# Which partitions the 64-feature rests are loaded into, in a linear-attention block with a gated feed-forward

## The chip, the cores and the metric

The kernel runs on one core of one Trainium2 chip. The metric is the device time of one execution in microseconds: 1095.71 us is the median of three runs before the change (1095.61 to 1099.36). The profile is of one further execution, taken by the hardware profiler.

## What is computed

x has 2048 tokens of 576 features. The reference, cut to what matters:

```python
xn = layernorm(x)
# A: linear attention, 32 heads of 18
q, k, v = split(xn @ wqkv)
pq, pk = phi(q), phi(k)             # phi(t) = t + 1 or exp(t), plus 1e-6
kv = einsum("bhsd,bhse->bhde", pk, v);  z = sum over s of pk
s = (pq @ kv) / (pq @ z + 1e-6) @ wo
# B: feed-forward, 576 -> 4608 -> 576
h = gelu(xn @ w1 + b1)
g = silu(h @ w2 + b2)
out = x + s * g
```

## The kernel before

Phase 1 (0 to about 190 us) normalizes x, multiplies it by wqkv and gathers the attention state. A hand-over (about 190 to 256 us) finishes the attention output of ten of the sixteen 128-token tiles and brings the main loop's first operands into SBUF. The main loop is the feed-forward, in two halves of 1024 tokens and, in each half, nine chunks of 512 hidden features. A short tail multiplies the last chunk and writes the output.

**Products.** Every large matrix product is made as seven block products with sums of blocks (the scheme of Strassen and Winograd); they are numbered 1 to 7 in the code. Each operand is held as a high part that the matmul unit takes exactly and a low part with what is left, so a product over 128 input features is three matmuls (high by high, high by low, low by high). The 576 input features of xn @ w1 are 4 x 128 and a rest of 64, which the block scheme cuts into two rests of 32. For a rest one matmul does all four combinations of high and low: 32 features x 2 parts of x x 2 parts of the weight fill the 128 partitions exactly. In class Up, product i of a pair of hidden blocks is six matmuls over X and a seventh whose moving operand is RX[:, RX_AT[i]] (the rest of x, 512 tokens wide) and whose stationary operand is a 128-column slice of we (the rest of w1); all seven are at line 1571 of the profile.

**The rests in DRAM.** The rests are split once, during phase 1 and the hand-over, and written to DRAM: rq_dram[half, i] holds for each product 32 features x (high, low) x 512 values, that is 64 rows of 2 KB; we_dram holds for each pair of hidden blocks 32 features x (high, low) x 896 values, rows of 3584 bytes. Each row goes to two partitions, so that each part of x meets each part of the weight. Before the change the upper 64 partitions of RX repeat the lower 64 (partition 64w + 2r + v holds feature r, part v of x), and the weights have part w in the 64 partitions from 64w on, each row on two neighbours. The tensor names in the profile are RX, we, rq_dram and we_dram.

**Who loads what, in which order.** All transfers are issued by SyncE (SP in the profile), one after the other in the order of the program; a transfer whose condition isn't met holds up all that are behind it. The engines' instructions are kept in the order written. The places that matter here:

- load_we (line 1346) issues two transfers of 224 KB for each pair of hidden blocks, 36 times. The first is called ahead of the hand-over's loop, right behind the load of w2raw (line 1301), the second in beside(7). In the main loop a table of steps (28 steps for each chunk) says when each call is made.
- load_rest (line 1455) is called from load_x_rest. In beside(5), within the hand-over, it is called for two tiles of RX and then for five; behind it stand the second load of w1raw (line 1362) and stores. At the change of half load_x_next loads for each of the seven products the X block of the second half (line 1888, 1 MB) and then its RX tile, one tile per call.
- load_q (line 1181) brings back a tile of q for the attention output: by_sums (line 1101, POOL) and p_mult (line 1116, POOL) work on it, then TensorE transposes (line 1252) and multiplies it (line 1287, ps_s).
- W1Loaded (line 1418) loads split blocks of w1 as wa, wc and wd in the second half; W2.load (line 1663) loads split blocks of w2, with one buffer each, so that its transfer waits until TensorE has done with the block of the chunk before (line 1733, pm).

Of the kernel before, what the change touches and what calls it, by code (L numbers as in the profile page):

```python
# [8 lines left out]
F32 = mybir.dt.float32  # L9
# [38 lines left out]
def linear_attention_gated_ffn(ctx, tc, x, xT, wqkv, wo, w1, w1e, b1, w2, b2, out):  # L48
    nc = tc.nc
# [65 lines left out]
    rq_dram = dram.tile([2, 8, 32, 2, 512], F32, name="rq_dram")  # L115
# [1222 lines left out]
    def load_we(n):  # L1338

        we_sb[n] = w1p.tile([P, WB, P], F32R, tag="we", name=f"we_{n}", bufs=2)  # L1340
        dst = we_sb[n].bitcast(F32).rearrange("p b c -> p (b c)")
        g, q = divmod(n % NP, WG)
        src = we_dram[q, 32 * g : 32 * g + 32]
        row = WB * P
        for w in range(2):
            nc.sync.dma_start(
                dst[64 * w : 64 * w + 64],
                bass.AP(
                    tensor=src.tensor, offset=src.offset + w * row,
                    ap=[[2 * row, 32], [0, 2], [1, row]],  # L1350
                ),
            )
# [97 lines left out]

    def load_rest(half, at, n, dst):

        src = rq_dram[half, at : at + n].rearrange("k r v c -> (r v) k c")
        for w in range(2):
            nc.sync.dma_start(dst[64 * w : 64 * w + 64].bitcast(F32), src)

    RX_AT = {i: at - (at > 2) for i, at in REST_AT.items()}

# [15 lines left out]
    def load_x_rest(half, i, n=1):  # L1474
        load_rest(half, REST_AT[i], n, RX[:, RX_AT[i] : RX_AT[i] + n])

    def beside(j):
        for half, what, *k in RESTS.get(j, ()):
            if half not in rests:
                rests[half] = Rest(half)  # L1480
            getattr(rests[half], what)(*k)
        if j == 2:
            nc.sync.dma_start(zb_dram, zb[0])
        if j == 4:
            w1t[0].hi("a"), w1t[0].lo("a")
        if j == 5:
            load_x_rest(0, 2, 2), load_x_rest(0, 4, 5)
            w1t[1] = W1(1)
            for i in (5, 6, 7, 4):
                w1t[0].T(i)  # L1490
        if j == 6:
            w1t[0].hi(6), w1t[0].lo(6)
            w1t[0].hi("c"), w1t[0].lo("c")
        if j == 7:
            load_we(1)
            w1t[0].hi("d"), w1t[0].lo("d")
# [9 lines left out]
    load_q(7)  # L1506
    w2_raw0.append(load_w2_raw(0))
    load_we(0)
    for j in range(NA):
        attend(j)  # L1510
# [541 lines left out]
    for step in range(n_chunks):  # L2052
        half, c = divmod(step, NC)
# [15 lines left out]
        if half == 0:  # L2069
# [7 lines left out]
            if (c, 5) not in w2_dram:  # L2077
                w = w2t[step]
# [5 lines left out]
        if not plain:  # L2084
            for k, at in enumerate((11, 16) if change else (8, 20) if step == NC else (7, 14)):
                add(base + at, load_we, 2 * step + 2 + k)
# [9 lines left out]
        elif not plain:  # L2096
            at = (11, 11, 16) if change else (7, 10, 24) if step == NC else (7, 14, 14)
# [7 lines left out]
            else:  # L2105
                make(W2, w2t, step + 1)

                w = w2t[step + 1]
# [42 lines left out]
        for j in range(CF // 2):  # L2151
            n = 2 * step + j
# [74 lines left out]
```

## Time and profile before

| | us |
|---|---|
| median of 3 runs | 1095.71 (1095.61 to 1099.36) |
| the profiled execution, its own time | 1107.71 |
| span in its profile, first to last instruction | 1105.9 |
| TensorE busy (PE) | 1084.5 |
| TensorE weight load busy (PEld) | 995.1 |
| VectorE busy (DVE) | 818.8 |
| ScalarE busy (ACT) | 524.8 |
| GpSimd busy (POOL) | 511.9 |

Mean granted TensorE clock 0.995; 258.63 MB moved, 234 GB/s in the mean. The profile has a page (busy time, the span in 40 slices, DMA queues, the chain of work that ended last, the costliest groups of instructions, DMA issues) and views that answer questions about the trace: waits, stretches of time, the chain in order of time, instructions in order of time. A line such as `PE a L1571 <- DMA wa<-op_a: 2.2, 1, 2.2` reads: TensorE, at line 1571, writing a, stood idle until a transfer from op_a to wa had landed; 2.2 us in all, once, 2.2 us the longest. `SPq` lines are the issues of transfers by SyncE; their time is that of the issue, not of the transfer. In the chain a `DMA` piece lasts from the issue to the landing.

### The profile page before, as it was taken

Reading aid. Unit: us, or ns where it says so; the run is one execution under the profiler, and the core shown is the slowest. Engines: PE = TensorE matmul, PEld = TensorE weight load, DVE = VectorE, ACT = ScalarE, POOL = GpSimd, SP = SyncE. Lnnn points to the kernel's source line nnn. Section 1 sums busy time; section 2 is a strip of 40 time slices with the busy share of each in tenths; the row PEclk is TensorE's granted clock in tenths of the full one; section 3 lists DMA queues with packets and bytes.
Section 4 is the critical chain, followed back from the end, with each engine's and each line's share of the span. In section 5 each row is a group of like instructions: output and inputs, shape, how many; then the busy total and the mean of one; then the engine's idle time right before and its main releaser. Section 6 shows DMA issues by size and latency. Waiting matters only on the chain.

```text
span 1105.9 us, 17916 instructions
## 1 busy us (share of the span) xinstructions
PE 1084.5 (98%) x6492; PEld 995.1 (90%) x6492; DVE 818.8 (74%) x1207; ACT 524.8 (47%) x872; POOL 511.9 (46%) x536
## 2 busy tenths in 40 slices
PE   8999999989999999999999998999999999999998
PEld 7999999788988989889899897989989899999988
DVE  6987763766898988989889884666747475664856
ACT  6756665635454554544545544244534434242442
POOL 3133241565585675765856743253334435252340
PEclk9999999999999999999999999999999999999999
DMA  6679733799577685685765799887767667676753
GB/s 235 192 277 230 232 117 134 248 339 350 193 245 283 205 299 204 224 291 199 283 243 202 262 290 338 290 273 230 219 208 225 200 212 224 186 236 207 233 157 137
DMA packets 91184, 258.63 MB, mean 234 GB/s; under 512 B 12246, under 2 KB 25558, under 8 KB 88792
## 3 DMA queue, kind: packets, MB, share of 16 engines
q1 hardware_dynamic: 91096, 257.49, 70.9%
q8 instruction: 51, 0.84, 0.3%
q14 instruction: 37, 0.30, 0.1%
HBM read 155.16 MB, written 101.40 MB: 232 GB/s over the span
## 4 chain that ended last, share of the span: by engine, by line
PE 89%; DMA 7%; ACT 2%; DVE 1%; POOL 1%; issue 1%; SPq 0%; POOLq 0%; DVEq 0%; ACTq 0%
PE pm L1733 32%; PE a L1571 10%; PE e L1571 10%; PE zy L1571 10%; PE b L1571 5%; PE x L390 4%; PE xaall L390 4%; PE pd L1854 2%; PE x1all L390 2%; PE psa L1287 2%; DMA X<-x_dram 1%; PE ps_kva L473 1%; DMA w2raw<-w 1%; PE x0all L390 1%; PE ps_s L1287 1%; PE xakv L390 1%
## 5 line engine op out<-in xcount | busy, mean ns | idle before, releaser
L1670 POOL TENSOR_TENSOR g<-g 128x256 f32<-128x256 f32 x204 | 185.4, 939 | 60.7 <-DVE h_l L1329 53.8
L1739 DVE TENSOR_TENSOR macc<-pm,macc 128x576 f32<-128x576 f32 x218 | 163.8, 751 | 47.7 <-PE pm L1733 47.2
L1326 ACT CAST h_h<-g 128x512 fp32r<-128x512 f32 x204 | 122.8, 621 | 123.3 <-PE pm L1733 122.2
L1329 DVE TENSOR_TENSOR h_l<-g,h_h 128x512 fp32r<-128x512 f32 x204 | 165.1, 816 | 2.4 <-ACT h_h L1326 2.3
L1571 PE MATMUL a<-X,wa 128*128 128x512 f32 x432 | 111.4, 394 | 2.2 <-DMA wa<-op_a 2.2
L1571 PEld LDWEIGHTS a<-X,wa 128*128 128x128 f32 x432 | 80.4, 190 | 18.1 <-ACT g L1579 2.6
L1588 ACT COPY mid<-a 128x512 f32<-128x512 f32 x36 | 21.1, 585 | 115.2 <-PE a L1571 115.2
L1670 POOL TENSOR_TENSOR mid<-g 128x256 f32<-128x256 f32 x68 | 52.2, 788 | 46.1 <-ACT g L1579 45.0
L1591 DVE TENSOR_TENSOR mid<-b,mid 128x512 f32<-128x512 f32 x36 | 24.8, 690 | 65.6 <-PE b L1571 59.0
L1377 POOL TENSOR_TENSOR w1raw<-w1raw 128x256 f32<-128x256 f32 x18 | 13.3, 741 | 117.1 <-ACT h_h L1326 71.6
L1579 ACT ACTIVATE g<-b,b1c 128x512 f32<-128x512 f32 x36 | 24.8, 689 | 66.9 <-DVE b L1597 66.9
L1571 PE MATMUL zy<-X,wd 128*128 128x512 f32 x216 | 55.0, 390 | 1.3 <-DMA X<-x_dram 1.3
L1571 PE MATMUL e<-X,wc 128*128 128x512 f32 x216 | 55.6, 392 | 0.0
L1571 PE MATMUL zy<-X,wc 128*128 128x512 f32 x216 | 54.8, 389 | 0.0
L1571 PE MATMUL e<-X,wd 128*128 128x512 f32 x216 | 54.8, 389 | 0.0
L1571 PEld LDWEIGHTS zy<-X,wd 128*128 128x128 f32 x216 | 40.5, 188 | 10.2 <-DMA X<-x_dram 1.7
L274 POOL TENSOR_TENSOR R<-R,bc 128x640 f32<-128x640 f32 x9 | 15.9, 1779 | 71.9 <-DMA R<-xT 48.5
L1571 PEld LDWEIGHTS zy<-X,wc 128*128 128x128 f32 x216 | 40.5, 188 | 8.4
L1571 PEld LDWEIGHTS e<-X,wd 128*128 128x128 f32 x216 | 40.5, 188 | 8.4
L1571 PEld LDWEIGHTS e<-X,wc 128*128 128x128 f32 x216 | 40.0, 188 | 8.3 <-DVE b L1597 0.3
L1579 ACT ACTIVATE g<-e,b1c 128x512 f32<-128x512 f32 x36 | 24.8, 690 | 45.3 <-DVE e L1604 45.3
L1329 DVE TENSOR_TENSOR h_l<-mid,h_h 128x512 fp32r<-128x512 f32 x34 | 36.0, 1059 | 1.2
(1018 smaller groups left out, 3190.9 us busy)
## 6 DMA issues: line engine op xcount, KB each, us to landing
we<-we_dram SPq DMA_DIRECT2D x72, 224.0 KB
w2raw<-w SPq DMA_DIRECT2D x10, 1152.0 KB
x_dram<-X SPq DMA_DIRECT2D x6, 1792.0 KB
w1raw<-w SPq DMA_DIRECT2D x18, 512.0 KB
op_a<-wa SPq DMA_DIRECT2D x18, 512.0 KB
op_c<-wc SPq DMA_DIRECT2D x18, 512.0 KB
op_d<-wd SPq DMA_DIRECT2D x18, 512.0 KB
wc<-op_c SPq DMA_DIRECT2D x18, 512.0 KB
```

Of the source, the lines that this page charges most:

```text
L390: nc.tensor.matmul(dst, st, w, start=start, stop=stop, skip_group_check=True)
L1287: nc.tensor.matmul(ps[:, h, :HD], st[:, k, :], w[v][k][:, h * HD : (h + 1) * HD], start=(i == 0), stop=(i == len(seq) - 1),)
L1326: nc.scalar.copy(pair[0], src)
L1329: eng.tensor_tensor(pair[1], src, pair[0].bitcast(F32), op=SUB)
L1571: nc.tensor.matmul(ps, st, mv, start=first and n == 0, stop=n == len(seq) - 1, skip_group_check=True,)
L1579: nc.scalar.activation(g, ps, AF.Gelu_apprx_tanh, bias=b1c[:, f : f + 1])
L1588: nc.scalar.copy(m1_sb, A)
L1591: tt(u1_sb, B, m1_sb, op=ADD)
L1670: nc.gpsimd.tensor_tensor(dst[:, cs], a[:, cs], b[:, cs], op=op)
L1733: nc.tensor.matmul(ps[:, q, :HD], hs[p][st][:, cs], m[:, p, :], start=(n == 0 and i not in CHAIN), stop=(n == 5), skip_group_check=True,)
L1739: nc.vector.tensor_tensor(dst, src, dst, op=ADD)
L1854: nc.tensor.matmul(ps, st[:, cs], w_all.rearrange("p n d -> p (n d)")[:, w], start=(i == 0), stop=(i == len(seq) - 1),)
```

## The change

Two loads put the same rows into other partitions, so that both operands of the rest matmul keep matching: partition 4r + 2v + w then holds feature r, part v of x, and in the weights feature r, part w. The weights still come in two transfers of 64 partitions each, but the first goes to all even and the second to all odd partitions. The rests of x come tile by tile in one transfer over all 128 partitions, whose source names each of the 64 rows twice in a row; there are as many transfers as tiles, where before there were two for each call (4 before and 7 after in the hand-over, 14 before and 7 after at the change of half). The bytes moved, the tensors in DRAM and all matmuls stay as they are.

```diff
@@ load_we
         for w in range(2):
             nc.sync.dma_start(
-                dst[64 * w : 64 * w + 64],
+                dst[w::2],
                 bass.AP(
                     tensor=src.tensor, offset=src.offset + w * row,
                     ap=[[2 * row, 32], [0, 2], [1, row]],
                 ),
             )
@@ load_rest(half, at, n, dst)
-        src = rq_dram[half, at : at + n].rearrange("k r v c -> (r v) k c")
-        for w in range(2):
-            nc.sync.dma_start(dst[64 * w : 64 * w + 64].bitcast(F32), src)
+        for k in range(n):
+            src = rq_dram[half, at + k]
+            nc.sync.dma_start(
+                dst[:, k].bitcast(F32),
+                bass.AP(tensor=src.tensor, offset=src.offset, ap=[[512, 64], [0, 2], [1, 512]]),
+            )
```

## The prediction

> **What bounds the kernel now.** I read the page first (busy shares, then the chain that ended last), then the busy time by stage, then what TensorE itself waited for, and only then the DMA rates of the stretches in which it waited.
>
> ```profile
> PE 1084.5 (98%) x6492; PEld 995.1 (90%) x6492; DVE 818.8 (74%) x1207; ACT 524.8 (47%) x872; POOL 511.9 (46%) x536
> ...
> PE 89%; DMA 7%; ACT 2%; DVE 1%; POOL 1%; issue 1%; SPq 0%; POOLq 0%; DVEq 0%; ACTq 0%
> ```
>
> TensorE (PE) is busy 98% of the span, and the chain is TensorE for 89% and a transfer for 7%. The change touches no matmul: it moves the same bytes by other descriptors. It can only earn what TensorE loses to late data, so the question is where that is.
>
> ```profile
> 190.00:256.00 66.00, 60.57 (x407) 55.25 (x406) 42.06 (x78) 31.88 (x64) 32.69 (x25) 0.97 0.85 282
> ...
> 300.00:525.00 225.00, 224.94 (x1333) 204.21 (x1333) 200.75 (x266) 112.40 (x195) 149.26 (x145) 1.00 0.68 244
> ...
> 640.00:680.00 40.00, 36.47 (x212) 32.57 (x211) 25.15 (x33) 18.27 (x25) 12.06 (x13) 0.96 1.05 306
> ...
> 760.00:1075.00 315.00, 313.29 (x1876) 285.10 (x1875) 194.33 (x279) 120.21 (x195) 125.77 (x138) 1.00 0.68 207
> ```
>
> Columns: stretch, its length, busy us of PE, PEld, DVE, ACT and POOL, then granted clock, busy share of the 16 DMA engines, GB/s. From 300 to 525 us TensorE is full (224.94 of 225 us): there the DMA engines have a third of their time free, and a faster or slower transfer changes nothing. It loses time in the hand-over before the main loop (190 to 256), at the change of half (640 to 680, where the DMA engines are more than full) and a little in the second half.
>
> ```profile
> PE ptp L1252 <- POOL pbuf L1116: 2.6, 2, 2.1
> PE a L1571 <- DMA wa<-op_a: 2.2, 1, 2.2
> ...
> PE zy L1571 <- DMA X<-x_dram: 1.3, 1, 1.3
> ...
> PE pm L1733 <- DMA w__8463<-op: 0.6, 1, 0.6
> PE pm L1733 <- DMA w__8969<-op: 0.6, 1, 0.6
> ...
> PE pm L1733 <- DMA w__10985<-op: 0.3, 1, 0.3
> ```
>
> Those are total us, times, longest. Three places have a transfer behind them. I call them A (change of half: 1.3 + 2.2 us), B (the 2.1 us wait for POOL, which itself waited for a load of q, below) and C (0.6 + 0.6 + 0.3 us in the second half).
>
> **The change part by part.** First the rate at which the transfers that it touches run now.
>
> ```profile
> 224.20:226.40 2.20, 1.31 (x10) 0.93 (x10) 2.14 (x4) 1.48 (x3) 2.20 (x2) 1.00 1.02 201
> 227.00:242.00 15.00, 12.89 (x98) 12.65 (x97) 9.34 (x20) 4.95 (x11) 7.28 (x6) 0.98 1.03 395
> 242.30:251.40 9.10, 9.10 (x62) 9.10 (x62) 3.91 (x7) 3.45 (x8) 5.11 (x6) 0.86 1.00 227
> 252.00:262.00 10.00, 10.00 (x54) 8.75 (x54) 3.92 (x7) 4.07 (x7) 3.10 (x3) 1.00 1.05 385
> ...
> 650.20:652.60 2.40, 2.40 (x20) 2.40 (x19) 2.40 (x5) 0.85 (x2) 0.00 (x0) 1.00 1.05 372
> ...
> 629.00:675.00 46.00, 42.47 (x255) 38.14 (x253) 35.39 (x46) 23.83 (x34) 19.60 (x20) 1.00 1.03 291
> ```
>
> The DMA engines are full in all six rows, yet the rate (last column) differs by a factor of two. At 242.3 to 251.4 the queue holds the rests of x for the first half (four transfers into 64 partitions each): 227 GB/s. Before and after them, with loads and stores over 128 partitions, it is 395 and 385. At 224.2 to 226.4, where the first rests of weights (two transfers, 64 partitions each) meet the tail of w2raw, it is 201. At the change of half it is 291 on average, with a short piece of 372 (650.2 to 652.6) that I take to be X loads alone. The full engines move little when a transfer fills half of the partitions.
>
> *A, rests of x.* load_rest for the second half issues 14 transfers of 128 KB (64 partitions, 2 KB each); after, 7 of 256 KB over all 128. Same bytes (1.8 MB). From 629 to 675 the queue moves 46 x 291 = 13.4 MB. At 372 GB/s, the row of X loads in pieces of the same 2 KB, that takes 36 us, so the last load that TensorE waits for lands 10 us earlier; if the rests of weights in it (four transfers of 224 KB) stay at 201, some 2 us of that are lost, leaving 8. What is needed:
>
> ```profile
> 651.73 13.69 DMA X<-x_dram
> ...
> 665.44 9.38 DMA wa<-op_a
> ...
> 674.96 3.32 PE a L1571 x7
> 678.28 1.69 PE b L1571 x7
> ```
>
> The chain goes through the X load of 651.73, whose landing let wa go at 665.44, and wa's landing let TensorE go at 674.96. The waits are 1.3 + 2.2 = 3.5 us, so 8 covers them twice. Behind the wait the matmuls run slow: 3.32 us for seven, then 1.69, where the same groups take 1.62 and 1.60 (rows below), 1.8 us together. With no wait that goes as well. A = 3.5 + 1.8 = **5.3 us**; nothing if the rests keep their rate. Next late after it is TensorE itself: the loads of w2 behind wa come earlier by the same shift. On SP seven issues go.
>
> *B, rests of weights ahead of q.*
>
> ```profile
> 228.26 9.93 DMA q<-q_dram
> ...
> 241.81 5.12 PE ps_s L1287 x28
> ...
> 247.48 7.46 PE ps_s L1287 x56
> 254.93 1.62 PE a L1571 x7
> 256.55 1.60 PE b L1571 x7
> ```
> ```profile
> 226.31 0.50 PE L1287 MATMUL ps_s<-kw_h,th 128*128 128x288 f32 x2 [0.89 <-DVE th L1258]
> ...
> 241.46 0.83 PE L1287 MATMUL ps_s<-kw_h,th 128*128 128x288 f32 x2
> ```
>
> ```profile
> 238.32 1.41 POOL L1101 TENSOR_TENSOR bs<-q,zb 128x576 f32<-128x576 f32 x1 [4.37 <-DMA q<-q_dram]
> ```
>
> This q landed at 238.2; POOL had waited 4.37 us for it, and POOL's product that TensorE needs comes behind it. It was issued at 228.26 when w2raw had landed, in the stretch of 201 GB/s. 2.2 us at 201 instead of 395 is 1.1 us lost. So the wait of 2.1 us can fall to 1.0. After the wait of 2.1, 28 matmuls took 5.12 us instead of 3.73 (half of 7.46), 1.4 us more; after one of 0.89 a pair took 0.50 and not 0.83, so a wait of 1.0 should cost little clock. B lies between 0 and 1.1 + 1.4 = 2.5. No row shows a transfer into every second partition: its nearest rows are 201 (half of the partitions) and 395 (spread over all), and they are equally near, so I take the middle, **1.2**. If the new spread collides more than the old one, B turns into a loss of about 1.1.
>
> [...]
>
> *C, rests of weights ahead of w2.*
>
> ```profile
> 783.06 1.16 SPq L1346 DMA_DIRECT2D we<-we_dram  x2
> 786.07 0.33 SPq L1663 DMA_DIRECT2D w__8463<-op  x1
> ```
> ```profile
> 786.07 6.82 DMA w__8463<-op
> ```
>
> In each step of the second half the two rest transfers go 3 us ahead of a w2 load that can start only when TensorE frees its buffer. It lands 6.82 us later, and TensorE waits in three of the steps, 1.5 us in all. C is between 0 and 1.5; middle again, **0.7**. Elsewhere in the main loop the 72 rest issues lie beside a full TensorE and count nothing.
>
> *First half, rests of x: three issues more.* The two calls at 238.65 issue 4 transfers now, 7 after.
>
> ```profile
> 238.65 4.26 SPq L1455 DMA_DIRECT2D RX<-rq_dram  x4
> ```
> ```profile
> L1455 SPq DMA_DIRECT2D RX<-rq_dram x18: 444/614/1486, 238.6 to 660.8; - x18
> ```
> ```profile
> L1346 SPq DMA_DIRECT2D we<-we_dram x72: 507/574/1864, 216.0 to 1030.9; - x72
> ```
>
> An issue that reads each row twice (L1346) takes 574 ns in the median, so seven are 4.0 us against 4.26 for the four: nothing between 0 and +1.7 (three at 574). Queued behind on SP are the second w1raw load, stores of s and of weights, and the next rests of weights; the rests themselves end by 251.4 and are first read at 256 (the last of the seven matmuls at 254.93), and at 227 GB/s or faster this margin only grows. Taken at 0. [...]
>
> **Sum:** 5.3 + 1.2 + 0.7 = 7.2 us less. The profiled execution took 1107.71 us for a span of 1105.9, so 1100.5. It stands 12.0 us over the median of 1095.71, and I can't tell where the timed runs save those 12. Taking the gain over unchanged: 1095.7 - 7.2 = **1088.5 us**, 0.66% less.
>
> **Rivals.**
>
> 1. *The gain isn't there: within 0.5%.* Either the 64 source rows, each feeding two partitions, are dealt out to the engines so that pairs still collide and the rests of x stay near 227; then A is 0 and B + C leave 1 to 2 us: 1094. Or the waits are smaller in the timed runs, which are 12 us shorter: half of the gain, 1092. For it: two of the three timed runs agree within 0.1 us, which is little for a kernel that waits on crowded transfers. [...]
>
> 2. *Slower: the second rest transfer waits for the first.* Before, the two went to partitions 0 to 63 and 64 to 127, apart from each other; now they interleave. If the ordering of writes takes them for overlapping, SP holds the second until the first has landed. Its place is C: at 783.06 the first would land some 6 us later (the 6.82 of the load behind it), so the w2 load would go at about 790 instead of 786.07, 4 us late, into a wait that has no slack in three steps. Seven steps by 3 to 4 us are 21 to 28 us, less A: **1115**. It decides as soon as a landing takes over about 3 us. Against it: the elements are disjoint, and nothing else in the trace shows such a wait.
>
> 3. *Slower: reading each row twice in a row halves the read.* If the rests of x then ran at half of 227, their 1.8 MB would take 8 us more, all of it in the waits of A: **1104**. Against: the rests of weights already read each row twice, and those issued at 248 us, behind the rests of x, pass within the stretch 252 to 262 at 385 GB/s.
>
> ```profile
> 248.00 1.49 SPq L1346 DMA_DIRECT2D we<-we_dram  x2
> ```
>
> **How the numbers follow.** Forecast (A whole, B and C from nothing to whole, 5.5 to 11 us): 0.56. Rival 1: 0.26. Rival 2: 0.11. Rival 3 and what else may slow it: 0.07. 0.5% (5.5 us) is about what a measurement of this kernel can tell from no change. So faster 0.56, within 0.26, slower 0.18. The range takes in the forecast and rival 1: from A, B and C whole (5.3 + 2.5 + 1.5 = 9.3) and 2 us more for what the sum of clock losses may hide, 1084.5, to no gain and most of the 1.7 of the added issues, 1097. That leaves out 0.18.
>
> **What would show it.** A right: rate from 629 to 675 near 370 instead of 291, no TensorE wait for X or wa, full clock after 675. B right: no dip to 201 near 225 and a PE wait for pbuf near 1 us. C right: the three waits for w2 gone. Rival 1: RX stretch still near 227 GB/s. Rival 2: gaps of several us between the two L1346 issues, with a transfer of we as releaser. Rival 3: RX stretch under 150. I am wrong in the main step if the RX stretch speeds up and the time still doesn't move: then the waits of A are the profile's own.

## The result, and the profile after

The changed kernel takes **1093.17 us** in the median of 19 runs (1092.51 to 1095.2). The kernel before, timed beside it, takes 1097.49 us in 19 runs (1094.30 to 1102.81). The ratio is 0.996 with a 95% interval of 0.9948 to 0.9972: 4.3 us less, where the prediction had 7.2 us less and 1088.5 us. The runs also scatter less: 2.7 us from end to end against 8.5.

The profiled execution after took 1094.21 us with a span of 1092.3 us, close to its own timed runs. That of before (1107.71) lies above all 19 timed runs of before. This difference between the two pairs, 13.5 us in the profiles and 4.3 us in the timed runs, is what the rest of this text is about.

The page of the changed kernel, busy time, chain by engine, and DMA queue 1:

```profile
PE 1078.4 (99%) x6492; PEld 990.5 (91%) x6492; DVE 822.8 (75%) x1207; ACT 524.6 (48%) x872; POOL 514.2 (47%) x536
...
PE 93%; DMA 2%; ACT 2%; DVE 1%; POOL 1%; issue 1%; SPq 0%; POOLq 0%; DVEq 0%; ACTq 0%
...
q1 hardware_dynamic: 91032, 257.49, 68.0%
```

The transfers' share of the chain fell from 7% to 2%, and TensorE is busy for 99% of the span. The same stages as before the change (columns as in the prediction: stretch, length, busy us of PE, PEld, DVE, ACT, POOL, then clock, DMA share, GB/s):

```profile
190.00:256.00 66.00, 62.03 (x421) 56.56 (x420) 43.95 (x81) 33.09 (x65) 34.40 (x27) 1.00 0.86 310
300.00:525.00 225.00, 224.94 (x1332) 204.26 (x1331) 201.41 (x267) 112.34 (x195) 149.31 (x146) 1.00 0.67 244
640.00:680.00 40.00, 39.99 (x230) 35.85 (x230) 29.03 (x40) 19.91 (x28) 12.32 (x13) 1.00 0.94 343
...
760.00:1075.00 315.00, 315.00 (x1916) 288.88 (x1915) 199.14 (x283) 121.25 (x196) 119.88 (x131) 1.00 0.65 211
```

At the change of half (640 to 680) TensorE is now full: 39.99 of 40 us at full clock, where it had 36.47 at 0.96. The second half is full too, 315.00 of 315. The stage from 300 to 525 us hasn't moved, as the prediction assumed. The stretches in which the changed transfers run, from the same view:

```profile
222.00:226.00 4.00, 3.11 (x23) 2.73 (x23) 3.84 (x7) 1.48 (x3) 3.01 (x2) 1.00 1.00 387
240.00:246.40 6.40, 6.40 (x51) 6.40 (x51) 3.73 (x7) 3.00 (x6) 4.81 (x5) 1.00 0.98 302
246.50:254.00 7.50, 7.50 (x47) 6.91 (x47) 0.12 (x1) 2.53 (x5) 0.00 (x0) 1.00 1.02 396
629.00:675.00 46.00, 45.99 (x272) 41.66 (x272) 34.33 (x47) 23.62 (x34) 17.89 (x20) 1.00 1.04 383
```

From 222 to 226 us, where the first rests of weights are loaded, the rate is 387 GB/s; over the same four microseconds it was 306 before, the dip to 201 included. The change of half runs at 383 GB/s instead of 291. The stretch with the seven rests of x in the hand-over (240 to 246.4) runs at 302: better than 227, short of the 372 and 395 of the rows that the prediction worked from. Behind it, 246.5 to 254, the rate is 396 (277 before). What TensorE waits for from 190 us to the end (total us, times, longest):

```profile
PE ptp L1252 <- POOL pbuf L1116: 1.3, 2, 0.9
PE ps_s L1287 <- DVE th L1258: 0.9, 1, 0.9
PE ptp L1252 <- POOL vb L1116: 0.8, 1, 0.8
PE ps_kw L1152 <- ACT kw L1159: 0.5, 1, 0.5
PE ps_s L1287 <- ACT th L1256: 0.2, 1, 0.2
PE ps_kw L1152 <- DVE kw L1157: 0.2, 1, 0.2
```

No transfer is among the releasers, and all six lines belong to the hand-over; in the main loop TensorE waits for nothing. The seven issues in the hand-over, in order of time on SP (start, duration):

```profile
235.96 5.64 SPq L1455 DMA_DIRECT2D RX<-rq_dram  x7
241.68 0.55 SPq L1362 DMA_DIRECT2D w1raw<-w  x1
```

They take 5.64 us where the four took 4.26. That difference needn't be the three issues' own: at the change of half of the same profile one issue of this line takes from 0.52 to 3.25 us. Code lines behind 1455 are three higher in the changed kernel, so 1574 is the line that was 1571.

**Where the 13.6 us between the two spans went.** I cut the chain (start, duration, what) at four points that both kernels pass: the start of the main loop, the ninth chunk (last of the first half), the eleventh chunk (behind the change of half) and the tail. The chain of the kernel before, the execution already profiled; its main loop starts at 254.93:

```profile
161.44 2.11 DVE X L299 x2
...
615.04 1.61 PE a L1571 x7
...
711.28 1.61 PE a L1571 x7
...
1075.30 25.80 PE pd L1854 x192
```

and of the kernel after:

```profile
160.04 2.11 DVE X L299 x2
...
250.77 1.62 PE a L1574 x7
...
610.83 1.61 PE a L1574 x7
...
700.45 1.61 PE a L1574 x7
...
1061.72 25.81 PE pd L1857 x192
```

In front of the main loop there are 4.2 us (254.93 - 250.77), of which 1.4 stand already at 160 us, ahead of everything that the change touches. The first eight chunks, up to the ninth, take 360.1 us in both. The change of half (ninth and tenth chunk) takes 96.24 before and 89.62 after, 6.6 us less; the eight chunks from there to the tail 364.02 and 361.27, 2.75 less. 1.4 + 2.8 + 6.6 + 2.75 is the 13.6 us. All three places of the prediction, A, B and C, are there, and in this pair of profiles all three are larger than I priced them (6.6 for 5.3, 2.8 for 1.2, 2.75 for 0.7). Yet the timed runs show 4.3 us. So the profiled execution of before was not what its timed runs do.

### The profile page after: what moved, and what is told of

Read it like the earlier page. It is cut to its first block, busy times and chain, and to the rows that moved or that the text cites. A ratio compares the mean times of both kernels' runs of the same rounds, so it can differ in the third digit from the quotient of the medians.

```text
span 1092.3 us, 17909 instructions
## 1 busy us (share of the span) xinstructions
PE 1078.4 (99%) x6492; PEld 990.5 (91%) x6492; DVE 822.8 (75%) x1207; ACT 524.6 (48%) x872; POOL 514.2 (47%) x536
## 4 chain that ended last, share of the span: by engine, by line
PE 93%; DMA 2%; ACT 2%; DVE 1%; POOL 1%; issue 1%; SPq 0%; POOLq 0%; DVEq 0%; ACTq 0%
PE pm L1736 35%; PE a L1574 11%; PE e L1574 10%; PE zy L1574 10%; PE b L1574 5%; PE xaall L390 4%; PE x L390 3%; PE pd L1857 2%; PE x1all L390 2%; PE psa L1287 2%; PE ps_kva L473 1%; PE x0all L390 1%; DMA w2raw<-w 1%; PE ps_s L1287 1%; PE xakv L390 1%; DMA q<-q_dram 1%
```

## The experiments

The expectations number three theories of this step (they are other ones than the prediction's rivals). Theory 1: the waits at A, B and C are real, but in most executions of before they are smaller than in the profiled one. Rival 2: A is worth nothing in the timed runs, and the gain comes from the rests of weights. Rival 3: the waits of the profile are the usual ones, and the changed kernel gives part of the gain back somewhere.

All times are medians. The kernel before was timed beside each group: 1098.56 us beside experiments 2, 5 and 6 and the first run of 3; 1097.34 beside the first two profiles of experiment 1 and the first two kernels of 4; 1097.42 beside the third profile and the repeated or last kernels of 3 and 4.

**1. The kernel before, three more times.** No edit; what matters is the profile.

> The kernel before once more, for its profile alone. Theory 1 (the losses at A, B and C vary from execution to execution, and the one profiled first was a bad one): a span of 1093 to 1102 us, with less than 9 us of waits and slow clock at the three places together, spread over them differently than the first time (A 5.3, B 3.5, C 1.5). If the losses are fixed by the program: 1105 us with the same waits to 0.3 us each.

> The same as the run before it, a second sample. Theory 1: the waits differ between the two samples by more than 0.5 us at one of the places at least. If the losses are fixed by the program: the same waits in both.

> The kernel before, a third extra profile. If the losses vary as in the two before it: 1 to 6 us more than the changed kernel at the change of half, 0.3 to 3 us more in the second half, and less than 1.5 us more at the start of the main loop.

They took 1096.36, 1101.1 and 1096.27 us. The chain of each, at the same cuts. First:

```profile
610.68 1.61 PE a L1571 x7
...
702.18 1.61 PE a L1571 x7
...
1063.97 25.80 PE pd L1854 x192
```

second, with the start of its main loop:

```profile
250.26 1.62 PE a L1571 x7
...
610.35 1.61 PE a L1571 x7
...
705.51 1.61 PE a L1571 x7
...
1068.71 25.81 PE pd L1854 x192
```

third, likewise:

```profile
250.83 1.62 PE a L1571 x7
...
610.93 1.61 PE a L1571 x7
...
701.71 1.61 PE a L1571 x7
...
1063.87 25.80 PE pd L1854 x192
```

| | main loop starts at | change of half (A) | from there to the tail (C) |
|---|---|---|---|
| before, the profile of the prediction | 254.9 | 96.24 | 364.02 |
| before, first | 250.6 | 91.50 | 361.79 |
| before, second | 250.3 | 95.16 | 363.20 |
| before, third | 250.8 | 90.78 | 362.16 |
| after | 250.8 | 89.62 | 361.27 |

Against after, A costs 1.9, 5.5 and 1.2 us in the three (mean 2.9), C 0.5, 1.9 and 0.9 (mean 1.1), and the hand-over nothing: the main loop starts as early as after the change. 2.9 + 1.1 = 4.0 us, close to the 4.3 us of the timed runs; with three executions that spread from 2.1 to 7.4 us, it can't be closer than that. The places are those of the prediction. The kind of the waits is in part: the second execution names X, wa and two loads of w2, the third only wa, the first no transfer; what those two still lose behind the change of half is put down to ScalarE's h_h (0.4 and 0.5 us). In the second one, from 605 to 1070 us, TensorE waits for:

```profile
PE zy L1571 <- DMA X<-x_dram: 2.3, 1, 2.3
PE a L1571 <- DMA wa<-op_a: 1.3, 1, 1.3
PE pm L1733 <- DMA w__9475<-op: 0.6, 1, 0.6
PE pm L1733 <- DMA w__10482<-op: 0.6, 1, 0.6
PE pm L1733 <- ACT h_h L1326: 0.3, 2, 0.2
```

and its TensorE instructions in order of time (start, duration, what, in brackets the idle time before and its releaser) show what such a wait does beside itself:

```profile
661.53 1.52 PE L1571 MATMUL a<-X,wa 128*128 128x512 f32 x6
...
667.20 2.76 PE L1571 MATMUL zy<-X,wd 128*128 128x512 f32 x6 [2.33 <-DMA X<-x_dram]
...
671.73 1.60 PE L1571 MATMUL a<-X,wa 128*128 128x512 f32 x6 [1.34 <-DMA wa<-op_a]
```

Behind the wait of 2.33 us six matmuls take 2.76 us instead of 1.52; behind that of 1.34 they take 1.60. Between these two the cost (1.24 and 0.08 us) grows faster than the wait. In the third the wait for wa is 0.9 us; in the first the wait (1.6 us) is put down to ScalarE's g, but wa had been issued 9.4 us earlier, about as long as it takes to land in the others (9.38, 9.92 and 9.87), so the profile doesn't separate the two there. Theory 1 holds. Rival 2's main point falls: A costs something in all four executions of before.

**2. Only the loads of x.** The changed kernel with the weights put back:

```diff
-                dst[w::2],
+                dst[64 * w : 64 * w + 64],
```

> The new loads of x alone; the rests of weights stay in halves of the partitions, so the two rests no longer match and the share of the last 64 input features of xn @ w1 comes out wrong. Theory 1 (the three waits are real, but in most executions of the kernel before they are smaller than in the one that was profiled; the change of half, A, holds most of them): 2 to 4 us less than before, no wait for X or wa in the profile, the dip near 225 us and the waits for w2 still there. Rival 2 (in most executions A is nothing, and what is gained comes from the rests of weights): within 1 us of before. Rival 3 (the profiled waits are the usual ones, and the changed kernel gives some of the gain back elsewhere): 5 us less or more.

1095.9 us (12 runs), ratio 0.997 (0.9952 to 0.9988): 2.7 us less, as Theory 1 has it. Two stretches, the change of half and the second half:

```profile
629.00:675.00 46.00, 45.98 (x272) 41.68 (x271) 34.15 (x46) 23.97 (x35) 18.67 (x20) 1.00 1.04 360
700.00:1050.00 350.00, 348.77 (x2103) 318.50 (x2102) 220.91 (x313) 135.17 (x219) 139.52 (x158) 1.00 0.71 220
```

A is gone (89.65 us, 45.98 of 46 busy). In the second half 1.2 us are still lost, and the DMA engines are busy for 0.71 of the time. I had expected named waits for w2 there; there is none in this profile, and the 1.2 us are waits for VectorE's h_l and ScalarE's h_h (0.9 and 0.2).

**3. Only the weights.** The kernel before with the one line of load_we changed. Run twice.

```diff
-                dst[64 * w : 64 * w + 64],
+                dst[w::2],
```

> The new loads of weights alone; the rests of x stay in halves, so that here too the share of the last 64 input features comes out wrong. Theory 1: 0.5 to 2.5 us less than before; the wait of 2.1 us for pbuf falls to about 1 and the waits for w2 are gone, the waits for X and wa stay. Rival 2: 3.5 to 4.5 us less. Rival 3: 2.5 to 5 us less.

> All rests of weights in the new layout and the rests of x in halves, once more. Theory 1 as it now stands (either half of the change alone brings enough at the change of half, and only the weights bring the second half's 1 to 2 us): 4 to 6 us less than before, its slowest execution below 1096; waits at the change of half below 1 us.

1093.64 us (7 runs), ratio 0.9938 (0.9914 to 0.9962), and again 1093.78 (7 runs), 0.9959 (0.9944 to 0.9974). That is the whole gain. The first run's 4.9 us are more than the 0.5 to 2.5 that Theory 1 had for it, and Theory 1 was wrong that the waits for X and wa would stay; here Rival 2's number (3.5 to 4.5) was nearer. The first one's stretches:

```profile
629.00:675.00 46.00, 45.74 (x270) 41.13 (x270) 33.84 (x46) 23.49 (x34) 17.56 (x19) 1.00 1.05 336
700.00:1050.00 350.00, 350.00 (x2111) 319.82 (x2111) 221.51 (x314) 135.16 (x219) 139.81 (x158) 1.00 0.67 221
```

The second half is full, with the DMA engines busy for 0.67 of the time instead of 0.71 at nearly the same rate (221 and 220 GB/s). And A is gone as well (90.16 us, in the second run 89.64; the one wait left is 0.2 us for wa), though the 14 transfers of rests of x still go into halves. 336 GB/s are enough there. Either part alone removes A, so the two gains don't add; only the weights bring C.

**4. Which of the weights.** In the kernel before, the new spread for some of the 36 pairs only: n < 2 is the hand-over, n >= NP the second half, from the change of half on. Each of the three kernels has one of the + lines.

```diff
-                dst[64 * w : 64 * w + 64],
+                dst[w::2] if n < 2 else dst[64 * w : 64 * w + 64],     # hand-over
+                dst[w::2] if n >= NP else dst[64 * w : 64 * w + 64],   # second half
+                dst[w::2] if n < 2 or n >= NP else dst[64 * w : 64 * w + 64],   # both
```

> The new layout for the rests of weights of the first two pairs of hidden blocks only (those loaded in the hand-over); the other 34 and the rests of x stay in halves, so the share of the last 64 features is wrong for the first two pairs. Theory 1 with the loss of typical executions in B: 2 to 4 us less than before, the dip near 225 us gone. If it lies at A or in the second half: within 1 us of before.

> The new layout for the rests of weights of the second half only (18 of 36 pairs, from the change of half on); all else as before, so the share of the last 64 features is wrong in the second half. Theory 1 with the loss of typical executions in B: 0 to 2 us less than before, the dip near 225 us still there. If it lies at A or in the second half: 3 us less or more.

> The rests of weights of the second half alone in the new layout, once more, on the same chip as its two neighbours. If B is worth 1 to 2 us in the mean of many executions: 1 to 2 us over the kernel with all rests of weights new. If B was the first execution's own: within 1 us of it.

> The new layout for the rests of weights of the hand-over and of the second half; only the 16 pairs that the main loop of the first half loads, and the rests of x, stay in halves (the share of the last 64 features is wrong where the two differ in layout). If the loads of the first half's main loop cost nothing: the time of the kernel with all rests of weights new, within 1 us. If the hand-over costs nothing either (all profiles since the first show its wait for pbuf below 1 us in either layout): the same as with the second half alone, too, within 1 us.

| new spread in | us (runs) | ratio and interval | A | C |
|---|---|---|---|---|
| the hand-over | 1098.24 (12) | 1.0002 (0.9982 to 1.0023) | 91.56 | 364.13 |
| the second half | 1095.38 (12) | 0.9976 (0.9957 to 0.9995) | 90.11 | 361.44 |
| the second half, again | 1093.88 (11) | 0.9964 (0.9952 to 0.9976) | 89.66 | 361.90 |
| both | 1093.76 (11) | 0.9963 (0.9951 to 0.9976) | 89.64 | 361.50 |

The hand-over alone brings nothing that can be measured (the interval leaves some 2 us either way), and adding it to the second half brings nothing either: the repetition of the second half, the two ends and the full set of weights (1093.78, above), timed together, lie within 0.2 us of one another. So B is worth nothing in the timed runs, and the second half alone brings the whole gain. This rests on the repetition: the first run of that kernel was only 2.0 us under before, which I had expected if the loss lay in B. In its profile A and C together are as small as in the repetition's, so why its timed runs were slower stays open. The stretches of the hand-over kernel:

```profile
629.00:675.00 46.00, 44.42 (x264) 40.11 (x263) 32.53 (x45) 22.17 (x33) 16.94 (x18) 1.00 1.05 319
700.00:1050.00 350.00, 347.67 (x2100) 317.65 (x2100) 220.92 (x314) 133.69 (x217) 136.51 (x157) 1.00 0.72 221
```

Here A and C are left, 1.6 and 2.3 us, 2.1 of the latter as waits for w2:

```profile
PE pm L1733 <- DMA w__8969<-op: 1.2, 1, 1.2
PE pm L1733 <- DMA w__7942<-op: 0.9, 1, 0.9
```

The DMA share from 700 to 1050 us sorts all fourteen profiles, at nearly the same rate (220 to 226 GB/s). With the weights of that half in halves (four of before, this one, x alone) the DMA engines are busy for 0.70 to 0.73, and with them on every second partition (eight, experiment 6 with all 128 at once among them) for 0.66 to 0.68. TensorE's losses overlap: the six lose 0.4 to 2.5 of the 350 us, in three of them behind loads of w2; of the eight, six lose nothing and two 0.4 and 0.8 us, behind VectorE and ScalarE and not a transfer.

**5. Spread, or 128 partitions in one transfer?** The changed kernel with the rests of x in two interleaved transfers, tiles together:

```diff
-        for k in range(n):
-            src = rq_dram[half, at + k]
...
+        src = rq_dram[half, at : at + n].rearrange("k r v c -> (r v) k c")
+        for w in range(2):
+            nc.sync.dma_start(dst[w::2].bitcast(F32), src)
```

> Both rests in two transfers, one to the even and one to the odd partitions, with the tiles of x together as before, so 4 issues in the hand-over and 14 at the change of half instead of 7 and 7. If what counts is only that each transfer is spread over all partitions: the time of the changed kernel within 1 us, and the rests of x move at 350 GB/s or more. If a transfer over 64 partitions is slower than one over 128 wherever they lie: 2 us or more over the changed kernel, rests of x below 300 GB/s.

1093.48 us (6 runs), ratio 0.9937 (0.9913 to 0.9961).

```profile
629.00:675.00 46.00, 45.98 (x272) 41.67 (x271) 34.33 (x47) 23.46 (x34) 17.90 (x20) 1.00 1.03 387
700.00:1050.00 350.00, 350.00 (x2112) 319.92 (x2111) 221.56 (x314) 135.17 (x218) 139.51 (x158) 1.00 0.68 221
```

387 GB/s against 383 from 629 to 675 us: two transfers into every second partition did as well here as one over all 128, where the four executions of before, with 64 neighbours in each transfer, have 283 to 325. What counts here is how the partitions lie, not how many one transfer has.

**6. The other way round.** Weights in one transfer over 128 partitions with each row twice in a row, rests of x in two interleaved ones for each tile:

```diff
+        nc.sync.dma_start(
+            dst, bass.AP(tensor=src.tensor, offset=src.offset, ap=[[row, 64], [0, 2], [1, row]]),
+        )
...
+            for v in range(2):
+                nc.sync.dma_start(
+                    dst[v::2, k].bitcast(F32),
+                    bass.AP(
+                        tensor=src.tensor, offset=src.offset + v * 512,
+                        ap=[[1024, 32], [0, 2], [1, 512]],
+                    ),
+                )
```

> The roles swapped: each rest of weights in one transfer over 128 partitions with each row twice in a row (36 issues instead of 72), the rests of x in two per tile to every second partition (14 and 14). Theory 1: the same as the changed kernel within 1 us, since what is left of its waits is not behind these transfers. If the issues on SyncE or the two-part load of weights still cost: 1 to 2 us less than the changed kernel.

1093.8 us (8 runs), ratio 0.9948 (0.9926 to 0.997); 380 GB/s at the change of half, A 89.75, C 362.21 with one wait of 0.8 us for ScalarE's h_h. None of the layouts tried gains more, and half the weight issues make no difference. In the hand-over, where the rests of x now take fourteen issues, the DMA engines are busy for only 0.83 of 240 to 254 us, at 281 GB/s; with the four issues of experiment 5 they are busy for all of it (1.00), at 359. Yet the main loop starts at 249.4, no later than in the others. No version beat the changed kernel beyond the intervals. The one line of load_we is enough for the whole gain; the rests of x have to follow it so that both operands of the rest matmul match, and which of these ways they are moved makes no difference to the time.

Rival 3 falls with all of this: the profiled execution of after agrees with its timed runs, it shows no wait that before didn't have, and the three extra profiles of before account for the timed difference without anything given back.

## Why the prediction was half right

- **What bounds the kernel, and where it loses:** right. TensorE lost time to late transfers at the change of half (named waits of 0.9 to 2.3 us) and, in some executions, in the second half (0.3 to 0.6 us each), and the main loop has no such wait now.
- **A:** right in place and mechanism. Predicted 5.3 us, 6.6 in that pair of profiles, 1.2 to 5.5 (mean 2.9) in three other executions of before. The rate came out at 383 where I had counted on 372. My 1.8 us of slow matmuls behind the wait belonged to an execution with a long wait; with the shorter wait for wa, 0.9 and 1.3 us, the seven take 1.86 and 1.83 us instead of 1.62. That the rests of x carry A was only half the cause: the rests of weights in the same queue, which I left at 201 GB/s, suffice alone (experiment 3).
- **B:** wrong as a gain. The rate does follow the layout: from 222 to 232 us it is 342 to 381 GB/s in the seven profiles with these weights in halves and 398 to 409 in the seven with them on every second partition (in experiment 6 on all 128 at once). But TensorE doesn't wait for it: the longest wait for pbuf is 0.5, 0.9 and 1.2 us in the three other executions of before, and 0.9 after. These three start their main loop as early as after does, and the hand-over's weights alone give 1.0002. The 2.1 us wait was that one execution's.
- **C:** right in size, 0.7 predicted within 0 to 1.5, and 1.1 in the mean (0.5 to 1.9), and right in that only the weights bring it. The waits behind it are only in part the predicted ones. The share that was a named wait for w2 varies from none to 2.1 us, so the 1.5 us of one profile were no upper end; the rest stands behind ScalarE and VectorE, and no run shows how the weights' layout reaches them.
- **Three more issues in the hand-over at 0:** right in effect. In the two profiles they cost SP 1.4 us (5.64 for 4.26), inside the 0 to 1.7, and no TensorE wait.
- **The step that failed** is "Taking the gain over unchanged: 1095.7 - 7.2". The sum was made from one execution that took 12.0 us longer than the median, and carried whole to runs that hadn't lost that time. The terms that were mis-sized by it are A, 2.9 in the mean instead of 5.3, and B, 0 instead of 1.2; with C at 1.1 the sum is 4.0 instead of 7.2. The prediction names the 12 us and says that it can't tell where they were saved. The extra profiles answer that in part: A, B and C themselves are smaller in the usual execution. The profiled one is the far end of a spread that the timed runs show too: of the 65 later timed runs of before, six took 1102.96 to 1105.82 us, three of them at a granted clock of 0.994 or 0.995, where most runs have 0.998 or more. The numbers at hand allowed a check: take all that A, B and C could be by the prediction's own upper ends, 9.3 us, from the profiled 1107.71 and 1098.4 is left, still above the timed median of 1095.71. So that execution had lost more than these waits against the timed runs, and nothing said that the waits themselves were not among what they had saved. The second branch of the first rival, waits that are smaller in the timed runs, half of the gain, is what came: 4.3 of 7.2, 0.4% and so within that rival's 0.5%.
- **The base:** the median of three runs, 1095.71, lay 1.8 us below that of the 19 runs, these three among them. 1093.17 - 1088.5 = 4.7 us is 1.8 of base and 2.9 of gain.
- **The second and third rival:** refuted. From 700 us on the 28 issues of load_we take 0.51 to 0.67 us each and none is preceded by a wait for a transfer of we; the stretches with the double reading of rows ran at 302 to 383 GB/s, not under 150. The argument against the third was weak, though: it took the row of 252 to 262 (385 GB/s) for rests of weights, where A takes the same row for transfers over 128 partitions. From 246.5 to 254 us, just behind the issue of those rests at 248, the same profile has 277.

What stays open: why the same kernel loses 1.2 us at A in one execution and 6.6 in another, and why its timed runs scatter over 8.5 us where those after the change scatter over 2.7: no run here shows a cause. Also open is why the first profile lost 1.4 us ahead of 160 us.

## What to carry to other kernels

Before a wait is priced from a profile, compare that execution's own time with the timed runs: if it lies far above them, the waits for transfers in it may be larger than usual (here 6.6 us at one place against 1.2 to 5.5), so price them over several profiles, or count only what the timed time can contain. Two edits that relieve the same crowded queue needn't add up: here the change of half takes 89.65 us with the loads of x alone, 90.16 and 89.64 with the weights alone and 89.62 with both. Ask of each whether it alone lifts the rate above what the waiting engine needs (here 336 GB/s were enough). And look at where in the partitions a transfer lands: here transfers into 64 neighbouring partitions kept the DMA engines busy for longer than those into 64 alternate ones (0.70 to 0.73 of the time from 700 to 1050 us against 0.66 to 0.68).

## What the runs showed of the hardware

- **Alternate partitions did as well as all.** From 629 to 675 us the rate is 387 GB/s with the rests of x in two transfers to every second partition, 383 with one over 128, and 283 to 325 in four executions with 64 neighbours each.
- **Transfers of the rests of weights into 64 neighbouring partitions kept the DMA engines busy for longer at nearly the same rate:** 0.70 to 0.73 of the time from 700 to 1050 us against 0.66 to 0.68 with the rests spread (220 to 226 GB/s in all). How long TensorE then waited for loads of w2 changed from one execution to the next, from nothing to 2.1 us.
- **Slow matmuls followed the long waits, hardly the short ones.** In the four executions of before the seven matmuls behind the wait at A lost 0.2 us where the wait was 0.9 to 1.6 us (1.83 to 1.86 for 1.62) and 1.7 us where it was 2.2 (3.32); the six behind a wait of 2.33 for X lost 1.24. Behind the wait of 0.2 us in experiment 3 the seven took 1.85 as well, so the 0.2 us didn't grow with the wait, from 0.2 to 1.6 us.
